# A chunked state recurrence with a squared-ReLU layer behind it: R loaded in runs of four tokens and turned on TensorE, the second correction in an accumulator of its own, the last decay row by an exponential, and a new order of all work

## The chip, the core and the metric

One core of one Trainium2 chip runs the whole program. The metric is device time in microseconds (us) of one execution. A core has five engines that work beside each other, each through its own list in order: TensorE (PE, with PEld for its weight loads), VectorE (DVE), ScalarE (ACT), GpSimd (POOL) and SyncE (SP, which here only issues DMAs). Sixteen DMA engines move the data that SP and POOL ask for.

## What is computed

For each of 4 batches and 8 heads a 40 x 40 state runs over 768 tokens, and each token's read-out goes into a two-matrix layer:

```python
for t in range(S):
    y[:, :, t] = np.einsum('bhd,bhde->bhe', rt, state)
    Sa = np.einsum('bhde,bhe->bhd', state, at)
    state_decay = state * wt[:, :, None, :] - np.einsum('bhd,bhe->bhde', Sa, bt)
    state = state_decay + np.einsum('bhd,bhe->bhde', vt, kt)
...
x = attn_out.transpose(0, 2, 1, 3).reshape(B * S, H * D)
out = np.maximum(x @ w_in, 0.0) ** 2 @ w_out
```

Inputs and output are float32; r, k, v, w, a, b are (4, 8, 768, 40), w_in is (320, 2048), w_out (2048, 320) and out (3072, 320).

## The kernel before

**Tiling.** The 768 tokens are cut into 6 chunks of 128. A *part* m = 0 to 23 is one chunk of one batch (m = 4c + batch) with all 8 heads; a *step* st = 0 to 47 is half a part (4 heads); a *unit* n = 0 to 47 is a quarter of the first matrix's work on two parts' tokens (in the groups of `SPLIT`, half of that on one part's); an *output* n = 0 to 23 is the 128 x 320 result of one part. Within a chunk the recurrence is done with triangular matrices in bf16; between chunks a state is handed on per batch.

**One part, in the order of its data.**

- Loads (`load`, L80 to L87): W, A, K, B, V and R of a part, each 160 KB as 128 tokens x 8 heads x 40 numbers, so in runs of 160 bytes. K and B share a tile NKB, R and V share NRV. Each tile has 4 buffers (`AHEAD`), and SP issues the loads in the order written.
- Decays: ln of W (`b_ln`, ACT), running sums on TensorE (`b_cs`), then exp of minus the sum (`b_xi`, GI), the sum less its own row (`b_cx`) and its exp (`b_gp`, GP). `b_gw` (L199) multiplies the last 32 token rows of W and GP on POOL or DVE; TensorE picks the last row out of that (`last_decay`).
- Scaled operands: `b_pk` (K and B times GI), `b_pa` (A times GP) into KBAp, and `b_cv` (L211, R and V cast to bf16 into RVp).
- Turning: K, B, A, R and V are needed with tokens along the free axis. For K and B this is done on TensorE in parts 0 to 19 (`b_kt`, 8 turns of 128 x 128, moved out by `b_kv`), for A in parts 0 to 7 (`b_ta`), for R and V in parts 0 to 7 (`b_rm`, 8 turns, moved out by `b_rv`). What is left goes by a DMA transpose that SP issues: `b_ka` (L252: A alone, 4 blocks, in parts 8 to 19, all of K, B and A, 12 blocks, in parts 20 to 23) and `b_rt` (L229: R and V, 8 blocks, parts 8 to 23).
- The solve: `st_a_mm` makes the triangular matrices, `st_a_ev` and `st_a_cut` move them out of PSUM and cut them (by a mask on DVE, or a copy on ACT and a cut on POOL). `b_p` starts an accumulator P, `b_m` moves it out, a first correction (`k1`) is added into P, `b_c1` takes the difference, a second correction (`k2`) is added into the same P, and `b_sn` moves the result out as SN. `b_x` (two POOL operations, L361 and L362) works out the size of the second correction for a check, `b_jk` and `st_energy` sum squares for that check on ACT.
- The read-out: `b_t`, `st_ex_mm`, `st_ex_ev` (EX), `st_z`, `st_kb` (uy), `st_y` (YN), `st_u` (the state handed on), `b_xt` and `b_xv` (the part's tokens turned for the layer, XS).

**The layer.** `f_r` and `f_m` (L543) multiply XS by w_in (WIN, loaded by POOL in ten pieces, `load_win`, two of which SP copies to a second half of the partitions, `twin_win`, L509); `f_e` (L563) takes the ReLU, `f_q` squares, `f_o` (L578) multiplies by w_out, `f_v` and `f_w` move the output out and store it.

**The end.** `sums` (L601) adds up the squares on TensorE, `verdict` (L605 to L618, DVE) compares them with bounds, and `get_flag` (L622) reads one flag into every engine; a branch (L885) follows. Two outputs (22 and 23) are moved out and stored behind the branch (`LAST`); the other side of the branch is a slow general path.

**The order.** Nothing is scheduled by the program's framework. `ORDER` is a text of some 1,900 tokens; each token issues one piece of work (`a.8@e1` is `st_a_mm` of step 8 into the PSUM banks e and 1, `pk.6:P` is `b_pk` of part 6 on POOL). The order of tokens gives the order on every engine, after a colon stands the engine, after @ the PSUM bank.

Of the kernel before, what the change touches and what calls it, by code (L numbers as in the profile page):

```python
# [18 lines left out]
def kernel(  # L19
# [62 lines left out]
    def load(key, m):  # L82
# [5 lines left out]

    NHC = 2 * NCH
    AN, AM, AC, AG, AI = 0, NBC, NBC + NHC, NBC + 2 * NHC, 2 * NBC + 2 * NHC  # L90
# [9 lines left out]
            for key, n in (("KBA", 4), ("G", 3), ("RV", 4))}  # L100
# [7 lines left out]
    def fill(k):  # L108
# [3 lines left out]
        elif k == 4:  # L112
            eng.memset(HM[:], 0.0)
            for u in range(2):
                eng.memset(HM[64 * u:64 * u + 64, :, u:u + 1], 1.0)
        elif k < 16:
            key, i = (("KBA", k - 5) if k < 9 else ("G", k - 9) if k < 12 else ("RV", k - 12))
            eng.memset(pads[key][i][:] if key == "G" else pads[key][i][:, :, :, D:64], 0.0)
        elif k < 19:
            eng.memset(SNs[k - 16][:, :, :, D:64], 0.0)  # L120
        else:
            eng.memset(UZs[k - 19][:], 0.0)
# [23 lines left out]
    HOME = {"f": {"tag": "ff", "bufs": 2}, "0": {"tag": "ca0"}, "1": {"tag": "ca1"},  # L146
# [51 lines left out]
    def b_gw(m):  # L198
        engine("gw", m).tensor_tensor(out=bt[m].G[LAST_T, 0, :, 0:D], op=ALU.mult,  # L199
                                      in0=nat.pop(("W", m))[LAST_T, 0], in1=bt[m].GP[LAST_T])  # L200
# [10 lines left out]
    def b_cv(m):  # L211
        move(pick["cv", m][0], bt[m].RV[:, :, :, 0:D], nat.pop(("RV", m))[:])
# [66 lines left out]
    CNs, Ps, TBs, uys, Mc, Cc, XSs = {}, {}, {}, {}, {}, {}, {}  # L279
# [26 lines left out]
    def cut_off(by, t_):  # L306
        if by == "A":
            nc.gpsimd.affine_select(  # L308
                out=t_, in_=t_, pattern=[[0, 2], [0, 2], [1, L]],
                compare_op=ALU.is_gt, fill=0.0, base=0, channel_multiplier=-1)  # L310

    def st_a_cut(st, s):
        cut_off(pick[f"av{s}", st][0], CNs[st][:, :, s])
# [22 lines left out]
    def b_m(m):  # L336
        c, bb = divmod(m, NB)
        if bb == 0:
            Mc[c] = chp.tile([128, NQ, 4, D], BF16, name="Mc", tag="Mc")
            Cc[c] = chp.tile([128, NQ, 4, D], BF16, name="Cc", tag="Cc")  # L340
        move(pick["m", m][0], part(Mc, m), flat(Ps[m]), -1.0)

    def corr(m, X, last):
        for h in range(NHH):
            nc.tensor.matmul(out=Ps[m][:, h // 2, h % 2, 0:D],  # L345
                             lhsT=CNs[m, "b"][:, h // 4, h // 2 % 2, h % 2, 1, :], rhs=X[:, h],
                             start=False, stop=last, skip_group_check=True)

    c1s = {}
# [5 lines left out]

    def b_sn(m):
        move(pick["s", m][0], flat(SNs[m % NSN]), flat(Ps.pop(m)), -1.0)

    def b_x(m):
        t_ = qdp.tile([128, NHH, D], FP32, name="x1", tag="x1", bufs=2)  # L360
        nc.gpsimd.tensor_tensor(out=t_[:], in0=part(Mc, m), in1=c1s.pop(m)[:], op=ALU.add)  # L361
        nc.gpsimd.tensor_tensor(out=part(Cc, m), in0=t_[:], in1=flat(SNs[m % NSN]), op=ALU.subtract)  # L362
# [7 lines left out]
    def st_energy(su):  # L370
        if su < 0 or su % 2 == 0:
            return
        hc = su // (NQ // 2)
        c, q = divmod(hc * (NQ // 2), NQ)
        src, at = ((Mc, AM), (Cc, AC))[su % (NQ // 2) // 2]
        jm = qdp.tile([128, NQ // 2, 4, D], BF16, name="jm", tag="jm", bufs=1)
        nc.scalar.activation(out=jm[:], in_=src[c][:, q:q + NQ // 2], func=ACTF.Square,
                             accum_out=ACC[:, at + hc:at + hc + 1])
# [43 lines left out]
    def st_ex_cut(st, s):  # L422
        cut_off(pick[f"ev{s}", st][0], EXs[st][:, :, s])
# [69 lines left out]
    def b_xv(m):  # L493
        c, b_ = divmod(m, NB)
        if b_ == 0:
# [25 lines left out]
    def unit(n):  # L521
        if n not in units:
# [3 lines left out]
            if jj == 0:  # L526
                Gts[h] = chp.tile([128, HB, NJ, L] if h in SPLIT else [128, NJ, HB, L], BF16,
                                  name="Gt", tag="Gt")
            if h in SPLIT:
                o.j0, o.per, o.bs = 8 * (jj % 2), 4, slice(b0 + jj // 2, b0 + jj // 2 + 1)  # L530
                o.Gt = Gts[h][:, jj // 2].rearrange("p j (a b) -> p j a b", a=1)
            else:
                o.j0, o.per, o.bs = 4 * jj, 2, slice(b0, b0 + HB)
                o.Gt = Gts[h][:]
            o.hp = [ps.tile([128, o.per, 4 // o.per, L], FP32, name="hp", **bank("fr", n, u))
                    for u in range(2)]
            o.begun = [0, 0]
        return units[n]

    def ffn_mm(o, u, i, g, rows):  # L540
        j = o.j0 + o.per * u + i
        o.begun[u] += 1
# [23 lines left out]
    def f_q(n):  # L566
        o = units[n]
        hs = o.hs[:].rearrange("p u x -> p (u x)")
        engine("q", n).tensor_tensor(  # L569
            out=o.Gt[:, o.j0:o.j0 + 2 * o.per].rearrange("p j a b -> p (j a b)"), in0=hs, in1=hs,  # L570
# [25 lines left out]
    def last_energy():  # L596
        st_energy(NS - 1)

# [4 lines left out]
    def verdict():  # L603
# [3 lines left out]
        nc.vector.memset(ok[:], 1.0)  # L607
        nc.vector.tensor_scalar(out=ok[:, AN:AN + NBC], in0=es[:, AN:AN + NBC], scalar1=1.5,
                                scalar2=None, op0=ALU.is_le)
        nc.vector.scalar_tensor_tensor(out=ok[:, AM:AM + NHC], in0=es[:, AM:AM + NHC],  # L610
                                       scalar=2.0 ** -16, in1=es[:, AC:AC + NHC],
                                       op0=ALU.mult, op1=ALU.is_ge)
# [8 lines left out]
    def get_flag():  # L621
# [4 lines left out]
        f.1:D lW.0 f.2:P lA.0 w.4@x w.11@0 f.4:D lW.1 f.20:D f.0:D f.9:D w.8@u lK.0 ln.0 f.16:D  # L626
# [292 lines left out]
```

## Time and profile before

| | |
|---|---|
| three runs, us | 257.33, 255.94, 257.05 (median 257.05) |
| the profiled execution, first to last instruction (its span) | 255.8 us |
| TensorE busy | 240.2 us (94%) |
| VectorE, ScalarE, GpSimd busy | 201.4, 206.3, 203.5 us |
| DMA | 184,467 packets, 38.44 MB, mean 150 GB/s |
| first matmul of the layer / last one | 38.7 us / about 251.3 us |

The profile gives no time for the profiled execution but its span; the median of the three runs lies 1.25 us above that span. Busy times are unions of instruction spans, so a busy share says how long an engine had something in it. Matmuls overlap one another in their spans. Of SP only what it issues and waits for is told.

### The profile page before, as it was taken

How to read it: one execution, taken by the hardware profiler on the slowest of the kernel's cores; microseconds unless marked ns; L12 is line 12 of the kernel's file. 1: busy time of each engine (PE TensorE's matmuls, PEld its weight loads, DVE VectorE, ACT ScalarE, POOL GpSimd, SP SyncE). 2: the span in 40 equal slices, each digit the busy share in tenths (PEclk: the TensorE clock that was granted, in tenths of full speed). 3: DMA queues.
4: the chain of work that ended last, by engine and by line, in shares of the span. 5: the costliest groups of instructions: out<-in, count | busy, mean ns of one | idle time of the engine just before them, and what ended most of it. 6: DMA issues, size and time to landing. Idle time of an engine off the chain costs nothing.

```text
span 255.8 us, 9549 instructions
## 1 busy us (share of the span) xinstructions
PE 240.2 (94%) x3893; PEld 193.8 (76%) x3893; DVE 201.4 (79%) x429; ACT 206.3 (81%) x470; POOL 203.5 (80%) x231
## 2 busy tenths in 40 slices
PE   7896787999999999999999999999998999799995
PEld 3464575899888888888888788888886877687872
DVE  4887798599999889899798898879797877575450
ACT  3598899499979898978999887889997868759821
POOL 6489787779989979999999999898896894197500
PEclk9999999799999999999999999999999999999999
DMA  7999998999988989999999977999999999540011
GB/s 130 189 153 187 166 180 149 168 168 163 169 157 153 155 146 163 164 186 190 148 171 172 201 137 142 166 152 209 150 158 162 186 179 130 118 120 28 28 55 62
DMA packets 184467, 38.44 MB, mean 150 GB/s; under 512 B 180064, under 2 KB 183136, under 8 KB 184416
## 3 DMA queue, kind: packets, MB, share of 16 engines
q1 hardware_dynamic: 183072, 35.14, 82.6%
q0 software_dynamic: 1344, 2.62, 6.1%
q8 instruction: 32, 0.52, 0.8%
q14 instruction: 19, 0.16, 0.2%
HBM read 28.84 MB, written 3.93 MB: 128 GB/s over the span
## 4 chain that ended last, share of the span: by engine, by line
PE 69%; DMA 15%; POOL 6%; SPq 5%; issue 2%; ACT 1%; DVE 0%; POOLq 0%
PE hp L543 20%; SPq L85 5%; DMA KBT<-KBAp 5%; PE cs L174 4%; PE ca L288 4%; PE ex L411 4%; PE tt L219 3%; PE uy L457 3%; PE P L345 2%; DMA WIN<-in_moe_w_in_dram 2%; DMA RV<-RVp 2%; PE uy L452 2%; DMA NA<-in_a_dram 2%; DMA WIN<-WIN 2%; DMA NKB<-in_b_dram 2%
## 5 line engine op out<-in xcount | busy, mean ns | idle before, releaser
L543 PE MATMUL hp<-XS,WIN 128*128 128x256 bf16 (+3 forms) x720 | 73.5, 255 | 2.0 <-DMA WIN<-WIN 2.0
L563 ACT ACTIVATE hs<-hp 128x512 bf16<-128x512 f32 x96 | 55.6, 600 | 15.7 <-PE hp L543 14.2
L543 PEld LDWEIGHTS <-WIN 128*128 128x128 bf16 (+1 forms) x720 | 49.6, 115 | 8.3 <-issue 3.6
L303 DVE TENSOR_TENSOR CN<-ca,MEX 128x512 bf16<-128x512 f32 x60 | 39.5, 683 | 8.8 <-PE ca L288 8.2
L578 PEld LDWEIGHTS <-Gt 128*128 128x128 bf16 x384 | 35.2, 97 | 12.3 <-issue 0.3
L303 DVE TENSOR_TENSOR EX<-ex,MEX 128x512 bf16<-128x512 f32 x60 | 39.9, 683 | 4.2 <-PE ex L411 3.9
L569 POOL TENSOR_TENSOR Gt<-hs 128x1024 bf16<-128x1024 bf16 x21 | 40.4, 1928 | 0.6 <-ACT hs L563 0.3
L308 POOL TENSOR_SCALAR_AFFINE_SELECT CN<-CN 128x512 bf16<-128x512 bf16 x36 | 24.9, 698 | 10.9 <-ACT CN L301 7.8
L308 POOL TENSOR_SCALAR_AFFINE_SELECT EX<-EX 128x512 bf16<-128x512 bf16 x36 | 24.8, 703 | 6.6 <-ACT EX L301 5.1
L569 DVE TENSOR_TENSOR Gt<-hs 128x1024 bf16<-128x1024 bf16 x27 | 22.3, 830 | 5.3 <-ACT hs L563 4.5
L366 ACT ACTIVATE jk<-CN 128x1024 bf16<-128x1024 bf16 x24 | 25.6, 1068 | 0.2
L301 ACT ACTIVATE CN<-ca 128x512 bf16<-128x512 f32 x36 | 21.0, 594 | 4.9 <-PE ca L288 4.6
L203 POOL TENSOR_TENSOR KBAp<-NKB,GI 128x640 bf16<-128x640 f32 x14 | 22.2, 1582 | 2.1 <-DMA NKB<-in_b_dram 1.1
L208 POOL TENSOR_TENSOR KBAp<-NA,GP 128x320 bf16<-128x320 f32 x18 | 16.2, 900 | 7.2 <-ACT lnW L169 3.1
L301 ACT ACTIVATE EX<-ex 128x512 bf16<-128x512 f32 x36 | 20.6, 600 | 1.4 <-PE ex L411 1.1
L362 POOL TENSOR_TENSOR Cc<-x,SN 128x320 bf16<-128x320 f32 x24 | 20.1, 837 | 1.9
L457 PE MATMUL uy<-KBAp,EX 128*128 128x40 bf16 x384 | 21.3, 181 | 0.0
L288 PE MATMUL ca<-KBT 64*128 64x128 bf16 x384 | 17.9, 220 | 3.1 <-DMA KBT<-KBAp 2.1
L199 POOL TENSOR_TENSOR Gp<-NW,GP 32x320 bf16<-32x320 f32 x20 | 18.3, 920 | 2.9 <-issue 1.5
L361 POOL TENSOR_TENSOR x<-Mc,c 128x320 f32<-128x320 bf16 x24 | 20.0, 832 | 0.3
L473 DVE TENSOR_TENSOR YN<-uy,GP 128x224 bf16<-128x224 f32 (+1 forms) x48 | 16.5, 347 | 4.2 <-PE uy L457 4.2
L457 PEld LDWEIGHTS <-EX 128*128 128x128 bf16 x384 | 17.9, 96 | 0.9 <-issue 0.3
(151 smaller groups left out, 613.0 us busy)
## 6 DMA issues: line engine op xcount, KB each, us to landing
NW<-in_w_dram SPq DMA_DIRECT2D x24, 160.0 KB, 3.9
NA<-in_a_dram SPq DMA_DIRECT2D x24, 160.0 KB, 4.0
NKB<-in_k_dram SPq DMA_DIRECT2D x24, 160.0 KB, 4.0
NKB<-in_b_dram SPq DMA_DIRECT2D x24, 160.0 KB, 4.1
NRV<-in_v_dram SPq DMA_DIRECT2D x24, 160.0 KB, 4.0
NRV<-in_r_dram SPq DMA_DIRECT2D x24, 160.0 KB, 4.0
out_dram<-osb SPq DMA_DIRECT2D x24, 160.0 KB, 2.8
WOUT<-in_moe_w_out_dram POOLq DMA_DIRECT2D x2, 640.0 KB, 7.6
```

The lines of the kernel that those rows point to most:

```text
L203: engine("pk", m).tensor_tensor(out=bt[m].KB[:, 0:2, :, 0:D], in0=nat.pop(("KB", m))[:], op=ALU.mult, in1=bt[m].GI[:].rearrange("p (u h) e ...
L288: nc.tensor.matmul(out=ca[s][:, i, u, :], lhsT=o.KBT[half(s), u, j0 + i, :], rhs=o.KBT[half(s), 2, j0 + i, :], start=(i == 0 and u == 0), ...
L301: nc.scalar.activation(out=out, in_=in_[:], func=ACTF.Copy)
L303: nc.vector.tensor_tensor(out=out, in0=in_[:], op=ALU.mult, in1=MEX[:].rearrange("p (i u) x -> p i u x", u=2))
L308: nc.gpsimd.affine_select(out=t_, in_=t_, pattern=[[0, 2], [0, 2], [1, L]], compare_op=ALU.is_gt, fill=0.0, base=0, channel_multiplier=-1)
L362: nc.gpsimd.tensor_tensor(out=part(Cc, m), in0=t_[:], in1=flat(SNs[m % NSN]), op=ALU.subtract)
L366: nc.scalar.activation(out=jk[:], in_=CNs[m, "b"][:].rearrange("p x i s u t -> p (x i s) u t")[:, :, 1, :], func=ACTF.Square, accum_out=AC ...
L457: nc.tensor.matmul(out=uy[:, (2 * i + s) * D:(2 * i + s + 1) * D], lhsT=EXs[st][:, i, s, u, :], rhs=o.KB[:, u, 2 * (j0 + i) + s, 0:D], sta ...
L543: nc.tensor.matmul(out=o.hp[u][:, i], lhsT=inner(g, rows, j), rhs=XSs[o.c][rows, g, o.bs, :], start=(o.begun[u] == 1), stop=(o.begun[u] > ...
L563: nc.scalar.activation(out=o.hs[:, u], func=ACTF.Relu, in_=o.hp[u][:].rearrange("p j a b -> p (j a b)"))
L569: engine("q", n).tensor_tensor(out=o.Gt[:, o.j0:o.j0 + 2 * o.per].rearrange("p j a b -> p (j a b)"), in0=hs, in1=hs, op=ALU.mult)
L578: nc.tensor.matmul(out=ops[n][:], rhs=WOUT[:, j, :], lhsT=Gts[h][:, b_, j, :] if h in SPLIT else Gts[h][:, j, b_, :], start=(j == 0), stop ...
```

## The change

- **R.** R gets a tile of its own (NR) and is read by two DMAs of 80 KB, one for the even and one for the odd heads, in runs of four tokens (640 bytes). The partitions then hold (head pair, block of 32 token groups). `b_cr` casts it with a rearrangement, four TensorE turns per part (`b_rm`, now in all 24 parts) bring it to the layout needed, and `b_rv` moves it out with a second rearrangement. V alone is cast by `b_cv`; it is turned on TensorE in parts 0 to 6 (`b_vm`, `b_vv`) and by a DMA transpose of 4 blocks in parts 7 to 23.
- **Second correction.** It goes into a PSUM tile Q of its own. `b_xf` moves -P out in float32, `b_sn` subtracts Q from it on DVE (24 times), the check's sum of squares is taken from Q directly on ACT (`b_ec`, 24 of 320 columns), and `b_x` with its two POOL operations is gone. `b_em` keeps the sum of squares over the first move.
- **Last decay row.** `b_gw` is an exponential of 32 rows of the running sum on ACT, in all 24 parts. The tile of W is thereby free after `b_ln`.
- **K and B** are turned on TensorE in parts 0 to 15 (before: 0 to 19); from part 16 on K, B and A go by the DMA transpose of 12 blocks.
- **Cuts** (`aq`, `eq`) have an engine of their own in the order: 56 on POOL and 27 on DVE (before: 72 on POOL). Squares (`f_q`): 37 on POOL and 11 on DVE (before 21 and 27).
- **Order.** `ORDER` is another text; the PSUM banks of the tag `ff` are named one by one (f and g).

The diff, cut to its core:

```diff
+    def load_r(m):
+        c, bb = divmod(m, NB)
+        nat["R", m] = natp.tile([128, 2, TI, D], FP32, name="NR", tag="NR")
+        for s in range(2):
+            nc.sync.dma_start(
+                out=nat["R", m][:, s].rearrange("p i e -> p (i e)"),
+                in_=r[bb].rearrange("(j s) t e -> s j t e", s=2)[s, :, c * L:(c + 1) * L, :]
+                .rearrange("j (b i) e -> j b (i e)", i=TI))
...
     def b_gw(m):
+        if pick["gw", m][0] == "A":
+            nc.scalar.activation(out=bt[m].G[LAST_T, 0, :, 0:D], in_=bt[m].cs[LAST_T], func=ACTF.Exp)
...
     def b_cv(m):
-        move(pick["cv", m][0], bt[m].RV[:, :, :, 0:D], nat.pop(("RV", m))[:])
+        move(pick["cv", m][0], bt[m].RV[:, 1, :, 0:D], nat.pop(("V", m))[:, 0])
+
+    def b_cr(m):
+        move(pick["cr", m][0], bt[m].RV[:, 0].rearrange("p (i s) e -> p s i e", s=2)[:, :, :, 0:D],
+             nat.pop(("R", m))[:])
...
     def b_rm(m):
-        bt[m].t1 = turned(bt[m].RV, **bank("rm", m))
+        bt[m].t1 = turned(bt[m].RV, us=(0,), **bank("rm", m))
...
     def b_rv(m):
-        move(pick["rv", m][0], bt[m].RVT[:], bt[m].t1[:])
+        move(pick["rv", m][0], bt[m].RVT[:, 0].rearrange("p j (b i) -> p i j b", i=TI),
+             bt[m].t1[:, 0].rearrange("p i (j b) -> p i j b", j=PB))
...
         nc.sync.dma_start_transpose(
-            out=o.RVT[:].rearrange("p u j t -> p (u j) t"),
-            in_=o.RV[:].rearrange("p u h e -> p (u h e)"))
+            out=o.RVT[:, 1], in_=o.RV[:, 1].rearrange("p h e -> p (h e)"))
...
+    def b_xf(m):
+        x1s[m] = qdp.tile([128, NHH, D], FP32, name="x1", tag="x1", bufs=2)
+        move(pick["xf", m][0], x1s[m][:], flat(Ps[m]), -1.0)
+
+    def b_k2(m):
+        Qs[m] = ps.tile([128, PB, 2, 64], FP32, name="Q", **bank("k2", m))
+        corr(m, Qs[m], c1s.pop(m), True)
+
     def b_sn(m):
-        move(pick["s", m][0], flat(SNs[m % NSN]), flat(Ps.pop(m)), -1.0)
-
-    def b_x(m):
-        t_ = qdp.tile([128, NHH, D], FP32, name="x1", tag="x1", bufs=2)
-        nc.gpsimd.tensor_tensor(out=t_[:], in0=part(Mc, m), in1=c1s.pop(m)[:], op=ALU.add)
-        nc.gpsimd.tensor_tensor(out=part(Cc, m), in0=t_[:], in1=flat(SNs[m % NSN]), op=ALU.subtract)
+        nc.vector.tensor_tensor(out=flat(SNs[m % NSN]), in0=x1s.pop(m)[:], in1=flat(Qs[m]),
+                                op=ALU.subtract)
...
+    def b_ec(m):
+        energy(flat(Qs[m]), NHH * D, AC + m)
...
-        ep.0@f rb.44 o1.20@0 o2.21 q.44:D es.0 ov.21:D fa.47 ra.47 o2.20 o1.23@f rb.47 ov.20:D
-        o1.22@f q.47:D o2.22 o2.23 w.17@0 ow.21 ow.20 w.5@e w.18@s gw.21:P fl.0
+        q.46:D ra.47 q.47:P o1.22@e o2.22 o1.23@u o2.23 w.5@f ep.0@s ow.20 ow.19 w.18@x ov.21:A
+        ow.21 w.17@0 ow.18 es.0 fl.0
```

What this moves, at three places. **First, SP near the copies of w_in's pieces.** SP's list before (NA, NW, NKB, NRV are the parts' tiles, WIN1 the pieces that are copied):

```order
L85 DMA NA_612<-in_a_dram 128x8x40
L85 DMA NKB_625<-in_k_dram 128x8x40
L85 DMA NKB_625<-in_b_dram 128x8x40
L509 DMA WIN1_107<-WIN1_107 64x1024
L85 DMA NA_725<-in_a_dram 128x8x40
L85 DMA NKB_737<-in_k_dram 128x8x40
L85 DMA NRV_745<-in_v_dram 128x8x40
L85 DMA NKB_737<-in_b_dram 128x8x40
L509 DMA WIN1_107<-WIN1_107 64x1024
L85 DMA NRV_745<-in_r_dram 128x8x40
```

And SP's list now, at the same copies (NR is the new tile of R, NV that of V):

```order
L86 DMA NA_544<-in_a_dram 128x8x40
L86 DMA NW_546<-in_w_dram 128x8x40
L86 DMA NKB_548<-in_b_dram 128x8x40
L86 DMA NKB_548<-in_k_dram 128x8x40
L542 DMA WIN1_109<-WIN1_109 64x1024
L94 DMA NR_552<-in_r_dram 128x1x160 x2
L86 DMA NV_555<-in_v_dram 128x8x40
L94 DMA NR_557<-in_r_dram 128x1x160 x2
L542 DMA WIN1_109<-WIN1_109 64x1024
L86 DMA NV_561<-in_v_dram 128x8x40
```

The first copy stands behind 29 loads before and behind 33 now, four of these 33 being R's in two halves; between the copies stand four loads before and three now.

**Second, TensorE at the end.** Before, around the sums of squares (`ep`; Gt and WOUT belong to the second matrix, op_ is an output):

```order
L578 LDWEIGHTS Gt
L578 MATMUL op__6139<-WOUT,Gt 128x320
L601 MATMUL ep<-ACC,ones_f 1x96
L578 LDWEIGHTS Gt
L578 MATMUL op__6151<-WOUT,Gt 128x320
```

Now (`wu` is a filler matmul on ones):

```order
L610 MATMUL op__6377<-WOUT,Gt 128x320
L149 LDWEIGHTS ones_b
L149 MATMUL wu<-ones_b 128x512
L149 LDWEIGHTS ones_b
L149 MATMUL wu<-ones_b 128x512
L630 MATMUL ep<-ACC,ones_f 1x108
```

Before, 64 matmuls of the layer follow `ep` (56 of outputs 20 to 23 and 8 of a unit); now the last matmul of the last output stands ahead of it.

**Third, DVE at the end.** Before (`es` to `bad` is the check, `osb` an output moved out, TENSOR_LOAD the reading of the flag):

```order
L569 TENSOR_TENSOR Gt<-hs 128x1024 x5
L605 COPY es<-ep 1x96
L607 MEMSET ok 1x96
L608 TENSOR_SCALAR ok<-es 1x24
L610 SCALAR_TENSOR_TENSOR ok<-es 1x12
L613 TENSOR_SCALAR ok<-es 1x48
L616 TENSOR_REDUCE nok<-ok 1x1
L618 TENSOR_SCALAR bad<-nok 1x1
L158 COPY osb<-op__6139 128x320
L158 COPY osb<-op__6151 128x320
L569 TENSOR_TENSOR Gt<-hs 128x1024
L622 TENSOR_LOAD bad
```

Now:

```order
L170 COPY osb<-op__6242 128x320
L601 TENSOR_TENSOR Gt<-hs 128x1024 x2
L634 COPY es<-ep 1x108
L636 MEMSET ok 1x108
L639 TENSOR_TENSOR ec<-es 1x12
L640 SCALAR_TENSOR_TENSOR ok<-es,ec 1x12
L643 TENSOR_SCALAR ok<-es 1x24
L645 TENSOR_SCALAR ok<-es 1x48
L648 TENSOR_REDUCE nok<-ok 1x1
L650 TENSOR_SCALAR bad<-nok 1x1
L654 TENSOR_LOAD bad
```

The check has one operation more, and no work of the layer stands between it and the reading of the flag.

More of the change, by code (lines that the diff above doesn't have):

```diff
@@ L494, in b_xv @@
         c, b_ = divmod(m, NB)
[L495 removed]
+        if c not in XSs:
             XSs[c] = chp.tile([128, NG, NB, L], BF16, name="XS", tag="XS", bufs=3)
@@ L812 @@
     STEP = 8
+    held = [bank("o1", int(tok.split(".")[1].split(":")[0])) for tok in LAST.split()
+            if tok.startswith("ov.")]
+    spare = [x for x in HOME.values() if x not in held]
     def general():
```

391 lines of the change are left out of this document (199 added, 192 removed).

## The prediction

> **What bounds the kernel now.** I read the page's head, then the span cut into stages (columns: span, busy us and instructions of PE, PEld, DVE, ACT, POOL, then granted clock, DMA share, GB/s), then in each stage who waits and the chain that ended last.
>
> ```profile
> span 255.8 us, 9549 instructions
> 0.00:46.00 46.00, 37.06 (x558) 25.04 (x559) 35.36 (x81) 34.12 (x74) 34.19 (x55) 1.00 0.98 163
> 46.00:190.00 144.00, 143.71 (x2476) 121.66 (x2473) 126.20 (x267) 127.22 (x299) 133.67 (x139) 0.99 0.99 166
> 190.00:220.00 30.00, 26.82 (x451) 21.88 (x451) 22.10 (x45) 22.77 (x51) 20.50 (x25) 1.00 1.13 166
> 220.00:251.40 31.40, 31.39 (x411) 24.88 (x409) 17.71 (x40) 21.81 (x48) 15.12 (x15) 1.00 0.20 55
> 251.40:255.80 4.40, 1.23 (x6) 0.38 (x4) 0.00 (x0) 0.41 (x1) 0.00 (x0) 1.00 0.24 82
> ```
>
> Five stages. Up to 46 us PE is empty for 8.9 us, and much of the rest is filler, while the DMA engines are full (0.98): this stage ends when the data are in. From 46 to 190 us PE is never empty (143.71 of 144) and nothing shorter than PE's list can help, though DMA is full too (0.99) and POOL close (133.67). From 190 to 220 us PE is empty for 3.2 us with DMA over full. Up to 251.4 us PE works off the layer alone. The last 4.4 us are the end of the program. So only the first, third and last stage can give or take much, and PE's own work in between.
>
> In the first stage the chain and PE's waits read:
>
> ```profile
> 34.25 5.96 DMA WIN<-in_moe_w_in_dram
> 40.23 4.71 DMA WIN<-WIN
> ```
>
> ```profile
> PE hp L543 <- DMA WIN<-WIN: 2.0, 1, 2.0
> ```
>
> ```profile
> 45.50:49.00 3.50, 3.50 (x55) 3.45 (x53) 1.65 (x5) 1.62 (x4) 3.23 (x5) 0.51 1.09 189
> ```
>
> The layer waits 2.0 us for the second copy of a piece of w_in, and right behind it PE runs 3.5 us at a granted clock of 0.51, which loses 3.5 x 0.49 = 1.7 us.
>
> **R's loads.** What does a load cost where DMA is full?
>
> ```profile
> q1 hardware_dynamic: 183072, 35.14, 82.6%
> q0 software_dynamic: 1344, 2.62, 6.1%
> ```
>
> ```profile
> 240.00:256.00 16.00, 12.61 (x112) 8.80 (x109) 5.09 (x14) 5.34 (x12) 0.05 (x1) 1.00 0.14 48
> ```
>
> ```profile
> NRV<-in_r_dram SPq DMA_DIRECT2D x5, 160.0 KB, 4.7
> ```
>
> q1: 0.826 x 16 engines x 255.8 us / 183,072 = 18.5 ns for a packet of 192 bytes on average. A load of 160 KB in runs of 160 bytes is 1,024 packets: 1,024 x 18.5 / 16 = 1.18 us. No row shows 640 bytes. Below: 18.5 ns, 256 packets, 0.30 us a load. Above: by bytes at q0's price (0.061 x 16 x 255.8 / 1,344 = 186 ns for 1,949 bytes), 61 ns, 0.98 us. Nearest: from 240 us on almost only stores of 1,280 bytes run, 0.14 x 16 x 16 us for 48 GB/s x 16 us = 600 packets, so 60 ns. On the line between 192 bytes at 18.5 and 1,280 at 60, 640 bytes take 35.6 ns and a load of R 0.57 us. I take that: 0.61 us saved a load (0.20 to 0.88).
>
> The Trainium skill (DMA: Bandwidth & Descriptors, "Specifications") says that transfers of 512 bytes and more go at line rate, about 27 GiB/s per engine. That would be 22 ns for 640 bytes, an estimate, 4.2 us instead of the 3.1 below, and 253.5 us in the end. The stores' 1,280 bytes in 60 ns (21 GB/s) do not reach that rate, so I stay with the line.
>
> *First stage:* five loads of R are issued by 46 us (row above), so the same data are in 5 x 0.61 = 3.1 us earlier (1.0 to 4.4). The copies of w_in now stand behind pieces that POOL asks for first, and ahead of the pieces that need no copy; that may take away the 2.0 us and with it the 1.7 us of half clock, or another first-time wait may take their place (0 to 3.7): half, 1.8 us. Together **-4.9** (-1.0 to -8.1).
>
> **Turns on PE.** Before: 20 x 8 for K and B, 8 x 4 for A, 8 x 8 for R and V, 256. Now: 16 x 8, 8 x 4, 24 x 4 for R, 7 x 4 for V, 284.
>
> ```profile
> 51.33 0.45 PE tt L219 x8
> ```
>
> 28 more at 0.45 / 8 = 56 ns are **+1.6** us on an engine that is never empty; nothing hides them. (Both ends: 0 if they fall into empty PE time before 46 us, 1.6.) The Trainium skill (TensorE: Matmul & The Clock Gate, "Part 4: PE-mode transpose") holds that turns don't count as busy for the clock and run at the slow one. By that the 28 would cost twice as much, an estimate of 3.1 us, and the end 256.1; but the row's 56 ns at granted clock 1.00 are 128 columns at full speed, so the trace speaks against it here.
>
> **The other engines** are not what ends the middle stage, so what they gain or lose costs nothing as long as they stay below PE. The prices:
>
> ```profile
> L569 POOL TENSOR_TENSOR Gt<-hs 128x1024 bf16<-128x1024 bf16 x21 | 40.4, 1928 | 0.6 <-ACT hs L563 0.3
> L362 POOL TENSOR_TENSOR Cc<-x,SN 128x320 bf16<-128x320 f32 x24 | 20.1, 837 | 1.9
> L199 POOL TENSOR_TENSOR Gp<-NW,GP 32x320 bf16<-32x320 f32 x20 | 18.3, 920 | 2.9 <-issue 1.5
> L361 POOL TENSOR_TENSOR x<-Mc,c 128x320 f32<-128x320 bf16 x24 | 20.0, 832 | 0.3
> ```
>
> ```profile
> L154 ACT ACTIVATE SN<-P 128x320 bf16<-128x320 f32 x18 | 7.9, 436 | 3.7 <-PE P L345 2.6 <-issue 1.0
> L377 ACT ACTIVATE jm<-Cc 128x640 bf16<-128x640 bf16 x12 | 8.8, 734 | 0.2 <-POOL Cc L362 0.2
> L180 ACT ACTIVATION_READ_ACCUMULATOR GI<-cs 128x1 f32 x24 | 5.0, 208 | 0.0
> ```
>
> POOL loses 40.1 (L361, L362) and 18.3 (L199) and gains 16 squares x 1.93 = 30.9: at least 27 us less, on the engine that was fullest in the middle. ACT gains 24 exponentials of 32 rows, priced like SN<-P (24 x 0.44 = 10.5), and 24 sums of squares (24 x 0.64 = 15.5), and loses 8.8 + 2.4 with jm<-Cc; the moves of casts and evictions nearly cancel. **ACT +14** in all, some 9.6 of it in the middle's 144 us (144 / 205 of the time after 46 us): 127.2 becomes 137, still under 144. I cost it at 0; what hides it is PE's list, and the cover is gone where ACT's 16.8 us of empty time can't be used (a rival). The second correction's own accumulator adds no matmul; its move and subtraction take the place of one move. A load of R is two issues now, but no longer shares a tile with V.
>
> **Third stage.** PE's waits, and the pieces of the chain:
>
> ```profile
> PE ca L288 <- DMA KBT<-KBAp: 2.1, 2, 1.4
> PE ex L411 <- DMA RV<-RVp: 1.1, 1, 1.1
> ```
>
> ```profile
> 188.66 5.88 DMA RV<-RVp
> 202.99 6.36 DMA KBT<-KBAp
> 213.40 5.26 DMA KBT<-KBAp
> ```
>
> All 3.2 us of empty PE are DMA transposes that land late in a full queue. R no longer goes that way (4 blocks instead of 8), the queue carries 24 x 0.61 = 14.6 us less up to there, but K, B and A go by 12 blocks from part 16 instead of 20. Between 0 and all of the 3.2, nearer to all: **-2.4** (-3.2 to +3.2, the rise if the eight full transposes each wait as the last four do).
>
> **The end.** Rows of PE, DVE, ACT and of the flag's readers:
>
> ```profile
> 242.85 0.33 PE L601 MATMUL ep<-ACC,ones_f 128*1 128x96 f32 x2
> 244.52 0.24 DVE L605 COPY es<-ep 1x96 f32<-1x96 f32 x1
> 245.55 0.14 DVE L618 TENSOR_SCALAR bad<-nok 1x1 int32<-1x1 f32 x1
> 250.08 1.25 PE L578 MATMUL op__6200<-WOUT,Gt 128*128 128x320 bf16 x8
> 251.37 0.44 ACT L154 ACTIVATE osb<-op__6200 128x320 f32<-128x320 f32 x1 [0.60 <-PE op__6200 L578]
> 251.17 1.46 PE L137 MATMUL wu<-ones_b 128*128 128x512 bf16 x6
> ```
>
> ```profile
> L622 ACTq TENSOR_LOAD <-bad x1: 464/464/464, 245.9 to 245.9; - x1
> L622 SPq FUSED_REGOPS  x1: 183/183/183, 248.5 to 248.5; - x1
> ```
>
> Before, the check lay under the last outputs, and the last copy out began 0.04 us behind the last matmul (250.08 + 1.25 to 251.37). Now everything stands in a row behind it: two fillers (2 x 1.46 / 6 = 0.49), `ep` 0.33, `es` to `bad` 245.69 - 244.52 = 1.17 and one operation more (0.17), the flag 0.46, the branch about as long as SP's 0.18, then output 22's copy (0.44), which waits behind the branch too, ahead of the last one: 3.24 - 0.04 = **+3.2** (2.6 without the fillers' and branch's part, 4.0 with a wait between every two).
>
> **Sum** against the profiled span: 255.8 - 4.9 + 1.6 - 2.4 + 3.2 = 253.3. The median lies 1.25 above the span: **254.5 us**.
>
> **Rivals.**
> 1. *ACT becomes the bound of the middle.* For it: this wait of ACT can't be filled by more ACT work if the order has it at fixed places; ACT was already 88% full.
>
> ```profile
> ACT hs L563 <- PE hp L543: 14.2, 18, 2.8
> ```
>
> Against it: POOL, fuller still, left PE without a gap. If all 16.8 us of ACT's empty time stay, the middle takes 9.6 us longer: 262.9, as a time 264; it decides once more than 7.2 us (144 - 136.8) of empty time stay. Slower. 15%.
> 2. *The transposes of parts 16 to 23 wait twice as much*: the third term is +3.2 instead of -2.4: 260.1. Slower. For it the share of 1.13, against it the 14.6 us less in the queue. 12%.
> 3. *The longer runs are priced by bytes*, so the change hardly does what it says: five loads save 1.0 instead of 3.1 and the queue is as full in the third stage: 254.5 + 2.1 + 2.4 = 259.0. 12%.
> 4. *DMA, not PE, sets the pace all through* (share 0.98 and 0.99): then all 14.6 us come off and 255.8 - 14.6 + 1.6 + 3.2 + 1.25 = 247.3. Against it: PE without a gap for 144 us. 13%.
>
> **How the numbers follow.** The forecast, 252 to 257 us, has 48%. Half a per cent of 257.05 is 1.3 us, about what a measurement of this kernel can tell from no change, so faster is under 255.8 and slower over 258.3. Faster: three quarters of the forecast and rival 4, 0.48. Slower: rivals 1 and 2, most of 3, a little of the forecast, 0.34. The range leaves out half of rivals 1 and 4 and a little more: 247.5 to 261.5.
>
> **What would show it.** The first layer matmuls dense some 4 to 5 us sooner, and no half clock at 45 us; 284 turns; ACT near 220 us busy and POOL near 176; in the last 60 us waits of PE for KBT and RV well under 3.2 us; the check behind the last matmul and about 7.6 us from that matmul to the span's end. Wrong would be PE empty in the middle with ACT as the one waited for, R's loads landing no sooner, or a check that starts earlier than the list says.

## The result, and the profile after

The changed kernel takes **297.32 us** (median of 294.70, 295.51, 299.14 and 301.56) against 257.19 us before. Two of these four ran in a slower state (299.14 and 301.56 us), and every comparison from here on leaves such executions out, which makes 295.1 us here, 37.9 over before and a ratio of **1.147** (95% interval 1.138 to 1.156). Forecast were 254.5 us in a range of 247.5 to 261.5. The profiled execution has a span of 293.0 us, 37.2 more than before.

The page's head and first table:

```profile
span 293.0 us, 9683 instructions
PE 249.9 (85%) x3921; PEld 197.0 (67%) x3921; DVE 221.7 (76%) x466; ACT 227.0 (77%) x529; POOL 178.2 (61%) x192
```

No engine is full any more: PE falls from 94% to 85%, and none of the others has risen above the share that it had before. The stages (columns as in the prediction):

```profile
0.00:46.00 46.00, 34.82 (x455) 23.17 (x455) 31.61 (x79) 33.53 (x79) 29.01 (x50) 0.93 0.91 159
46.00:190.00 144.00, 128.50 (x2198) 105.23 (x2197) 121.03 (x255) 125.03 (x291) 95.33 (x99) 0.99 0.89 146
190.00:281.60 91.60, 84.92 (x1267) 68.21 (x1266) 67.85 (x126) 67.66 (x160) 53.89 (x45) 1.00 0.54 96
281.60:293.00 11.40, 1.65 (x8) 0.40 (x6) 1.18 (x8) 0.77 (x2) 0.00 (x0) 0.69 0.12 37
```

In the same 144 us of the middle PE starts 2198 matmuls instead of 2476 and is empty for 15.5 us instead of 0.3. The DMA share fell from 0.99 to 0.89.

Where the 37.2 us lie follows from two marks, the first matmul of the layer and the end of the last output's matmuls. Rows of the layer's tile and of the chain:

```profile
L571 PE MATMUL hp<-XS,WIN x720: 214/269/421, 44.0 to 275.9; 128*128 128x256 bf16 x72, 128*128 128x128 bf16 x48, 64*128 64x256 bf16 x36, 64*128 64x128 bf16 x24
```

```profile
279.40 2.17 PE op__6377 L610 x16
281.57 0.43 PE wu L149 x2
282.01 0.29 PE ep L630 x2
...
283.46 0.15 DVE bad L650
...
283.63 0.47 ACTq L654
...
284.16 0.05 ACTq L920
284.21 3.70 issue
...
288.05 0.06 ACT osb L166
```

The start takes 44.0 instead of 38.7 us (**+5.3**), the end 293.0 - 281.57 = 11.4 instead of 255.8 - 251.33 = 4.5 us (**+6.9**; 251.33 is 250.24 + 1.09 of before's last output), and what lies between 237.6 instead of 212.6 us (**+25.0**).

**The start.** The chain there:

```profile
12.55 5.20 DMA NR<-in_r_dram
18.52 1.50 POOL KBAp L218
20.05 0.54 ACT GI L192 x2
20.61 0.49 DVE cx L197
21.10 0.94 DVE KBT L170 x2
22.09 1.03 PE ca L313 x13
```

```profile
PE ca L313 <- DVE KBT L170: 6.0, 2, 5.4
```

```profile
22.00:24.00 2.00, 1.92 (x26) 1.32 (x27) 1.19 (x4) 1.06 (x4) 0.60 (x2) 0.50 1.34 182
24.00:26.00 2.00, 2.00 (x13) 1.26 (x12) 1.90 (x4) 1.60 (x3) 1.99 (x5) 0.50 1.40 172
```

R's first loads are needed early now, since R is cast on POOL ahead of part 2's scaling of K and B; that scaling waits in POOL's list, ACT's GI waits for a buffer that it frees, DVE's cx waits for GI, and PE stands for 5.4 us behind the move that follows cx. cx needs nothing of GI; both only read the tile cs, a pattern that returns in the middle. Behind the gap PE runs at a granted clock of 0.50 for 4 us. The half clock forecast to go from 45 us has moved to 22 us.

**The middle.** PE's own waits are short and many; what tells more are the waits of the engines that serve it, ACT and DVE:

```profile
ACT hs L591 <- PE hp L571: 5.2, 6, 2.1
ACT junk L397 <- DVE SN L392: 5.1, 3, 2.9
ACT x L166 <- DVE c L380: 4.7, 5, 2.2
```

```profile
DVE cx L197 <- ACT GI L192: 12.8, 5, 5.1
DVE SN L392 <- ACT junk L397: 5.1, 6, 1.9
DVE c L380 <- ACT x L166: 4.4, 5, 1.2
```

Before, ACT waited for PE (14.2 us at the layer). Now ACT and DVE wait for each other: `x` (-P in float32) and `c` only read P, and `junk` (the square) and SN only read Q, yet the two never run side by side on two engines. Rows of two places, ACT's and then DVE's:

```profile
86.77 0.43 ACT L397 ACTIVATE junk<-Q 128x320 bf16<-128x320 f32 x1
...
97.45 0.44 ACT L166 ACTIVATE x<-P 128x320 f32<-128x320 f32 x1 [0.77 <-DVE c L380]
```

```profile
87.32 0.49 DVE L392 TENSOR_TENSOR SN<-x,Q 128x320 bf16<-128x320 f32 x1 [0.55 <-ACT junk L397]
...
96.94 0.47 DVE L380 SCALAR_TENSOR_TENSOR c<-P,Mc 128x320 bf16<-128x320 f32 x1
```

SN begins 0.12 us behind the square's end, `x` 0.04 us behind `c`'s. In all 24 parts the square and SN stand at least 0.03 us apart, and so do `c` and `x` in the 18 where two engines do them. Which of the two waits goes by the order: SN begins behind the square in 8 of the 24 parts, and the square behind SN in 16; `c` behind `x` in 8 of the 18, `x` behind `c` in 10. So in 8 parts the change put a square of 0.43 us into the chain from Q to SN, which the diff doesn't say. The Trainium skill (PSUM — Partial Sum Buffer, "Terms") does: two engines may not be on one bank at once, reads against reads included. The trace agrees, with the waits above. The prediction did not weigh that rule.

DVE's largest wait is of the same kind: cx waits 12.8 us for GI, though both only read cs. Before, cx began ahead of GI in 21 of 24 parts; in the changed kernel it does so in 14.

Another thing in these lists is how long R's turned blocks take to move out:

```profile
L166 ACT ACTIVATE RV<-tt x19: 636/1329/1455, 24.0 to 239.2; 128x512 bf16<-128x512 bf16 x19
L170 DVE COPY RV<-tt x12: 408/1296/1339, 13.7 to 252.2; 128x512 bf16<-128x512 bf16 x12
```

```profile
L166 ACT ACTIVATE KBT<-tt 128x512 bf16<-128x512 bf16 x2 | 1.2, 590 | 0.0
L170 DVE COPY KBT<-tt 128x512 bf16<-128x512 bf16 x6 | 2.5, 418 | 0.9 <-PE tt L238 0.9
```

The first two rows give the shortest, middle and longest of 19 and 12 moves, 7 of them plain ones of V: 1.33 us on ACT and 1.30 on DVE in the middle. The same shape takes 0.59 us (ACT) and 0.42 us (DVE) in plain order. The Trainium skill (SBUF — State Buffer, "Door 1: The DMA port swizzle") holds that steps of up to 8 bf16 cost nothing; this move writes every fourth one and takes about twice as long on ACT and three times as long on DVE. If the step is what costs, page and measurement differ, and the measurement decides.

### The profile page after: what moved, and what is told of

It reads as the page before. It is cut to its first block, busy times and chain, and to the rows that moved or that the text cites. A ratio compares the mean times of both kernels' runs of the same rounds, so it can differ in the third digit from the quotient of the medians.

```text
span 293.0 us, 9683 instructions
## 1 busy us (share of the span) xinstructions
PE 249.9 (85%) x3921; PEld 197.0 (67%) x3921; DVE 221.7 (76%) x466; ACT 227.0 (77%) x529; POOL 178.2 (61%) x192
## 4 chain that ended last, share of the span: by engine, by line
PE 28%; ACT 24%; DVE 19%; issue 9%; SPq 7%; DMA 7%; POOL 5%; ACTq 0%; POOLq 0%; DVEq 0%
PE hp L571 7%; SPq L86 5%; ACT hs L591 5%; ACT RV L166 3%; DVE EX L328 3%; DMA NV<-in_v_dram 3%; DVE CN L328 3%; ACT jk L402 2%; ACT Gp L212 2%; ACT CN L326 2%; DMA NR<-in_r_dram 2%; PE ca L313 2%; POOL Gt L601 2%; ACT GI L192 2%; DVE RV L170 2%
## 5 line engine op out<-in xcount | busy, mean ns | idle before, releaser
L601 POOL TENSOR_TENSOR Gt<-hs 128x1024 bf16<-128x1024 bf16 x37 | 70.8, 1919 | 29.0 <-ACT hs L591 28.9
L591 ACT ACTIVATE hs<-hp 128x512 bf16<-128x512 f32 x96 | 54.6, 606 | 10.7 <-PE hp L571 5.2
L328 DVE TENSOR_TENSOR EX<-ex,MEX 128x512 bf16<-128x512 f32 x53 | 34.9, 684 | 4.6 <-PE ex L444 3.7
L218 POOL TENSOR_TENSOR KBAp<-NKB,GI 128x640 bf16<-128x640 f32 x17 | 26.8, 1574 | 11.1 <-PE uy L289 3.8
L333 POOL TENSOR_SCALAR_AFFINE_SELECT CN<-CN 128x512 bf16<-128x512 bf16 x26 | 17.1, 661 | 19.5 <-ACT CN L326 13.5
L326 ACT ACTIVATE EX<-ex 128x512 bf16<-128x512 f32 x43 | 25.2, 624 | 3.0 <-PE ex L444 3.0
L333 POOL TENSOR_SCALAR_AFFINE_SELECT EX<-EX 128x512 bf16<-128x512 bf16 x30 | 20.1, 677 | 12.2 <-ACT EX L326 6.5
L166 ACT ACTIVATE RV<-tt 128x512 bf16<-128x512 bf16 x19 | 24.1, 1266 | 0.1
L197 DVE TENSOR_TENSOR cx<-cs,lnW 128x320 f32<-128x320 f32 x24 | 11.6, 483 | 16.4 <-ACT GI L192 12.8
L313 PEld LDWEIGHTS <-KBT 64*128 64x128 bf16 x384 | 12.8, 96 | 15.4 <-DVE KBT L170 6.0
L186 PE MATMUL cs<-lnW,UTI 128*128 128x320 f32 x48 | 18.0, 460 | 0.7 <-ACT Gp L212 0.3
```

The costliest lines, as they stand in the source:

```text
L166: nc.scalar.activation(out=out, in_=in_, func=ACTF.Copy, scale=scale or 1.0)
L218: engine("pk", m).tensor_tensor(out=bt[m].KB[:, 0:2, :, 0:D], in0=nat.pop(("KB", m))[:], op=ALU.mult, in1=bt[m].GI[:].rearrange("p (u h) e ...
L313: nc.tensor.matmul(out=ca[s][:, i, u, :], lhsT=o.KBT[half(s), u, j0 + i, :], rhs=o.KBT[half(s), 2, j0 + i, :], start=(i == 0 and u == 0), ...
L326: nc.scalar.activation(out=out, in_=in_[:], func=ACTF.Copy)
L328: nc.vector.tensor_tensor(out=out, in0=in_[:], op=ALU.mult, in1=MEX[:].rearrange("p (i u) x -> p i u x", u=2))
L333: nc.gpsimd.affine_select(out=t_, in_=t_, pattern=[[0, 2], [0, 2], [1, L]], compare_op=ALU.is_gt, fill=0.0, base=0, channel_multiplier=-1)
```

## The experiments

All times are medians; "over" is the median less that of the kernel before in the same comparison. The changed kernel is 37.9 us over. It was timed in a comparison of its own, and the ratios' intervals are about 0.008 (2 us) to either side, so a difference between kernels of two comparisons is good to about 3 us, an estimate from these intervals.

**1. Is it R's rearranged move, the late check, R's runs, or ACT's load?** Four kernels, each the changed one with one edit.

```diff
 x1_flat
-        move(pick["rv", m][0], bt[m].RVT[:, 0].rearrange("p j (b i) -> p i j b", i=TI),
-             bt[m].t1[:, 0].rearrange("p i (j b) -> p i j b", j=PB))
+        move(pick["rv", m][0], bt[m].RVT[:, 0], bt[m].t1[:, 0])
 x2_early
-  fa.47 fa.46 o2.21 ra.46 rb.46 q.46:D ... o2.23 w.5@f ep.0@s ow.20 ... ow.18 es.0 fl.0
+  fa.47 ep.0@e fa.46 o2.21 ra.46 rb.46 es.0 q.46:D ... o2.23 w.5@f ow.20 ... ow.18 fl.0
 x3_short
-        natp.tile([128, 2, TI, D], FP32, name="NR", tag="NR")
+        natp.tile([128, 2, TI, D + 8], FP32, name="NR", tag="NR")
 x4_noec
-        energy(flat(Qs[m]), NHH * D, AC + m)
+        pass
```

> The changed kernel with R's turned blocks moved out in their plain order (the second rearrangement left out, so R's tokens stand in the wrong order and the output isn't the reference's; same bytes, same instructions). Theory A, the rearranged move: it takes 1.3 us instead of about 0.6 us, 24 times, on ACT (17) and DVE (7), and holds up everything behind it in two lists that are served in order. Then RV<-tt falls to about 0.6 us (ACT) and 0.42 us (DVE), 18 us of engine time go, and the span falls from 293 by 10 to 20 us. Theory B, the order: the new list couples the engines at fixed places whatever this move costs; the span stays above 288 us. Theory C, ACT's amount of work: ACT loses 12 of 227 us and the span falls by no more than 12 us.

289.18 us, ratio 1.120 (1.109 to 1.132), 30.6 over: **7.3 us** less. The moves fell to 0.61 (ACT) and 0.42 us (DVE), as theory A has it, but the span only to 287.5, 5.5 less than 293.0 and under A's 10 to 20. Theory C allows that too; x4 tests it.

> The changed kernel with the check's sums and the flag ahead of the last outputs, as before (all is computed). Theory: the end is a row of waits behind the last matmul: two fillers, sums, verdict, reading of the flag, and 3.7 us of branching that stood under the last outputs before. Then 7 us go, and from the last matmul of the last output to the span's end it takes about 4.4 us instead of 11.4. By the prediction's working the row is worth 3.2 us. Rival: the wait on the flag's branch stays exposed since the flag is read at the same place of each list, and under 1 us goes.

291.89 us, 1.127 (1.117 to 1.136), 33.3 over: **4.6 us** less. From the last output's matmuls to the span's end it takes 290.5 - 285.35 = 5.1 us instead of 11.4, 6.3 less. So the late row is worth 5 to 6 us, not 3.2. The difference is the branch, and it is TensorE's. Rows of the changed kernel, then one of before:

```profile
L920 ACTq COMPARE_BRANCH  x1: 50/50/50, 284.2 to 284.2; - x1
L920 PEldq COMPARE_BRANCH  x1: 3537/3537/3537, 284.2 to 284.2; - x1
```

```profile
ACT osb L166 <- PEq L920: 10.0, 1, 10.0
```

```profile
L885 PEldq COMPARE_BRANCH  x1: 3493/3493/3493, 250.2 to 250.2; - x1
```

ACT's own branch takes 0.05 us; the 3.70 us in its chain end when PE's sequencer is through its branch of 3.54 us. Before, that branch was as long, but ACT's two copies began at 250.33 and 251.37 us, ahead of its end. Why ACT's copies wait for it in the changed kernel was not separated.

> The changed kernel with R loaded in runs of 160 bytes again (each run goes to a slot of 48 numbers, so that no two join; all else as it is, all is computed). By the prediction a load of 160 KB costs 0.61 us more of the 16 engines in runs of 160 bytes than in runs of 640, 14.6 us in all: the share of the queue rises by about 5 points of the span, and the first stage ends about 3 us later. If the changed kernel's pace is set by engines that wait for one another and not by DMA, the time stays within 3 us; if it is set by the data, it rises by 5 to 15 us.

310.54 us, 1.203 (1.195 to 1.210), 52.0 over: **14.1 us** more. So R's longer runs are worth some 14 us in the changed kernel, though not in the way the prediction priced. The queue's rows:

```profile
q1 hardware_dynamic: 160896, 34.22, 69.0%
```

```profile
q1 hardware_dynamic: 179328, 34.22, 63.8%
```

That is 0.690 x 293.0 = 202 us of all 16 engines in the changed kernel and 0.638 x 308.4 = 197 us with 18,432 packets more: the queue's time has not grown. What has grown is SP's time for an issue, from 0.58 to 1.26 us in the median of 48:

```profile
L94 SPq DMA_DIRECT2D NR<-in_r_dram x48: 528/584/1992, 9.8 to 232.2; - x48
```

```profile
L94 SPq DMA_DIRECT2D NR<-in_r_dram x48: 543/1256/2868, 9.9 to 247.9; - x48
```

POOL's waits for R's data at its casts grow from 6.6 to 11.3 us. That this brings the 14 us was not separated.

> The changed kernel without the sum of squares over the second correction (24 squares of 128x320 and 24 readings of the sum on ACT, 16 us in all; the check then sees zeros). Theory C, ACT's amount of work bounds the kernel: the span falls by 12 to 16 us. Theory A or B: ACT is 77 per cent busy and waits in many places, so it falls by 2 to 8 us, less than by the plain move of R if A holds.

293.13 us, 1.135 (1.126 to 1.143), 34.6 over. 16 us less work on ACT bring 3.3 us, not told from nothing (the intervals overlap). ACT's amount of work, theory C, is not the bound.

**2. Is it the data, or the order?**

```diff
 y1_after_noload, y2_before_noload
+        if m >= AHEAD:
+            nat[pair, m] = held[pair, m % AHEAD]
+            return
 y3_reload (loads alone at other places, here part 10's of V; its cast is cv.10)
-  rt.9 lW.12 lV.11 ... lV.10 cv.10:P
+  z.12@x lV.10 fa.10 kb.12 k1.8 rm.9@s ... cv.10:P
 y4_before_r (before; R's path as in the change, part 8's tokens)
-  cv.8:A ... rt.8
+  cv.8:A cr.8:A ... rm.8@0 ... rv.8:D ... rt.8
```

> The changed kernel with the loads of parts 4 to 23 left out (their work is done on the data of parts 0 to 3, so the output isn't the reference's; 120 of 144 loads go, everything else stays in its place). Theory D, late data: the new list issues many loads only a few places ahead of the cast or scaling that needs them, and what waits for them on POOL, DVE and ACT is what PE waits for. Then nearly all of the loss in the middle goes: the span falls from 293 to 255 to 268 us. Theory B, the list's order on the computing engines: the span falls by less than 10 us.

297.26 us, 1.155 (1.148 to 1.161), 39.8 over: no gain. **Theory D falls**; the data of parts 4 to 23 does not set the changed kernel's pace.

> The kernel before with the same 120 loads left out (parts 4 to 23 work on the data of parts 0 to 3). By the prediction's reading PE is never empty from 46 to 190 us and only the third stage's 3.2 us and a part of the start are the data's: the span falls by 3 to 10 us. If data set the pace of before too (the prediction's fourth rival), it falls by 15 us or more.

252.46 us, 0.979 (0.973 to 0.984), 5.1 under. The 120 loads of parts 4 to 23 together are worth 5.1 us of before. This is the ceiling of whatever shorter loads of these parts could bring there, and it closes the fourth rival (247.3): in the middle the DMA share falls from 0.99 to 0.34.

> The changed kernel with SP's loads of parts 6 to 23 put at other places of the list: each as soon as its buffer is free, at most 90 places ahead of its first use (now 1 to 338 places ahead, several within 10); no other work is moved and all is computed. Theory D: the span falls by more than 10 us. Theory B: it stays within 5 us of 293.

303.13 us, 1.177 (1.169 to 1.184), 45.6 over: evenly placed loads cost 7.7 us more. Both theories missed it, and the cause is open; POOL waits less for loads, but ACT waits 8.0 us for W instead of 1.8.

> The kernel before, in its own order, with R's path of the change alone: R loaded in runs of four tokens into a tile of its own, cast and moved out with the two rearrangements, turned on TensorE in all parts (4 turns, put into gaps of the PSUM banks for parts 8 to 23; moved out by ACT in odd and DVE in even parts), V by the DMA transpose of 4 blocks. If R's path is itself the cost (rearranged moves, 64 more turns, a longer way from load to read-out), it takes 270 us or more. If the order is the cost (theory B or D), it stays within 254 to 264 us.

277.10 us, 1.074 (1.067 to 1.081), **19.6 over**. R's path alone, in the old order, costs 20 us as placed here, 3.2 of them ahead of the layer's first matmul (at 41.9 us, before at 38.7). PE's middle stage there:

```profile
46.00:190.00 144.00, 131.45 (x2257) 109.58 (x2254) 121.85 (x247) 120.01 (x275) 119.67 (x133) 1.00 0.82 142
```

DVE and ACT are no fuller in the middle than before (126.20 and 127.22), and still PE does 2257 matmuls instead of 2476: it is where the work stands and how long one piece holds its list, not the sum.

**3. The other parts alone, and all parts in the old order.** In z3 and z5 the fill of a buffer clears part 1's last decay row again, so part of the output isn't the reference's.

```diff
 z1_before_r_flat = y4 with x1's edit
 z2_second (before; part 10's tokens)
-  c.10 kb.18 k2.10 ... s.10:A ... x.10
+  xf.10:A c.10 kb.18 k2.10 ec.10 ... s.10
 z3_gw (before)
-  gw.3:P
+  xi.3 gw.3:A
 z5_all_old = y4 + z2 + z3, and for parts 16 to 19
-  kt.17@s kv.17:D ... ka.17
+  pa.17:P ka.17
```

> The kernel before with R's path of the change in its own order (as in y4), but R's turned blocks moved out in their plain order (the second rearrangement left out, so the output isn't the reference's). If the cost of R's path is the length of that move (1.1 to 1.2 us instead of 0.4 to 0.6, 24 times, on lists that PE waits for), most of the 20 us go: under 267 us. If it is what the path adds at all (72 turns, casts and moves at places where PE waits), it stays above 272 us.

267.23 us, 1.040 (1.027 to 1.052), 8.9 over, 10.7 less than y4. Just over half of R's path is the length of that one move.

> The kernel before, in its own order, with the second correction of the change alone (P moved out in float32 ahead of it by ACT, in six parts DVE; P's tile started anew; the difference on DVE; its square sums on ACT, 24 instead of 12; the two POOL operations gone). By the prediction it adds no matmul and costs nothing. If PE's density hangs on what DVE and ACT finish in time, the 24 moves and 24 squares on ACT (16 us more than went) cost something: 2 to 10 us.

279.06 us, 1.083 (1.069 to 1.097), **20.7 over**, far outside both guesses; 4.8 of them lie ahead of the layer's first matmul (at 43.5 us). As placed here, the second reader stands ahead everywhere: SN begins behind the square in all 24 parts, and `c` behind `x` in all 18 where two engines do them, against 8 and 8 in the changed kernel. (The second correction also reuses P's tile here instead of taking one of its own.) So this is the price of this placing, and not that of the part in the changed kernel. ACT waits at the square that stands right behind the correction, and SN waits for the square:

```profile
ACT junk L370 <- PE P L344: 18.3, 17, 3.5
...
DVE c L352 <- ACT x L154: 10.3, 9, 2.6
DVE SN L365 <- ACT junk L370: 6.9, 12, 1.0
```

PE's middle stage, with DVE and ACT less busy than before again:

```profile
46.00:190.00 144.00, 133.24 (x2293) 110.37 (x2291) 121.19 (x261) 117.40 (x284) 96.94 (x99) 1.00 0.93 155
```

> The kernel before, in its own order, with the last decay row by an exponential on ACT alone, right behind GI's (24 of 0.43 us; POOL and DVE lose 20 us). By the prediction it costs nothing. If ACT's list is what PE waits for, it costs 2 to 8 us.

259.99 us, 1.010 (0.994 to 1.026), 1.7 over: not told from nothing. One of its four executions took 566.11 us and is not in this median; its cause is open.

> All parts of the change but the new order, in the order of before: R's path (as in y4), the second correction (as in z2), the exponential (as in z3), and K and B by the DMA transpose from part 16 on. The cuts, the squares and the check at the end stand as before. If the new order is the cause of the loss in the middle, this takes 255 to 270 us. If the added work is, it takes 280 us or more, and at least the sum of y4, z2 and z3 over before.

311.34 us, 1.210 (1.197 to 1.223), 53.0 over: more than the changed kernel, and more than y4, z2 and z3 together (42.0). So the new order alone is not the cause, as **theory B** has it: the work added costs this much in the old order as placed here, 15.1 us more than in the new one. As z2 shows, the placing is itself an order; what the same work costs in the old order with the second readers behind was not tried.

**4. Taking the costs out of the changed kernel, one after the other.**

```diff
 w1_nosecond (with x4's edit)
-        x1s[m] = qdp.tile([128, NHH, D], FP32, name="x1", tag="x1", bufs=2)
-        move(pick["xf", m][0], x1s[m][:], flat(Ps[m]), -1.0)
-        nc.vector.tensor_tensor(out=flat(SNs[m % NSN]), in0=x1s.pop(m)[:], in1=flat(Qs[m]), ...
+        move("D", flat(SNs[m % NSN]), flat(Qs[m]), -1.0)
 w2 = w1 + x1's edit;  w3 = w2 + x2's edit;  w5 = z2 with x4's edit
 v1_noturn = w3, and rm and rv only for m < 4;  v2_noturn_noload = v1 + y1's edit
```

> The changed kernel without the second correction's extra readers: the move of -P in float32 and the sum of squares over Q are left out, and SN is taken from Q alone (so the output isn't the reference's); all matmuls and the order stay. Theory E, second readers: the profile shows that P and Q are never read by two engines at once (SN starts 0.03 us or more after the square's end in all 24 parts), so each second reader stands in the chain from P to SN, and what waits behind on PE, ACT and DVE with it. Then it falls from 297 to 275 to 285 us, far more than without the square alone (293). Rival, amount of work: ACT loses 24 of 227 us and DVE 3; no more than 8 us go.

290.36 us, 1.129 (1.121 to 1.137), 33.6 over: 4.3 us less, as the rival has it and not theory E's 12 to 22. What is expected above of all 24 parts holds for z2; in the changed kernel SN begins behind the square in 8, and there the second readers cost little.

> w1, and R's turned blocks moved out in their plain order too (as in x1). If the costs of the two parts add, 7 to 10 us less than w1. If one lies in the shadow of the other, less than 4 us.

285.47 us, 1.113 (1.106 to 1.119), 28.7 over: 4.9 less than w1, between the two guesses.

> w2, and the check ahead of the last outputs (as in x2): 5 to 7 us less than w2. What then is left over the 257 us of before is the new order, the 24 more turns with their banks, and the rest: under 268 us if the three parts are the cause, over 275 if most of it is something else.

280.38 us, 1.090 (1.085 to 1.096), 23.7 over: 5.1 less, and over 275: more than half is something else.

> The second correction alone in the old order (as in z2), without the sum of squares over the result (left out: the check sees zeros). Theory E: SN no longer stands behind ACT's square, and ACT no longer waits at it (18 us there in z2); of the 21 us that z2 lost 10 to 15 go: 264 to 269 us. Rival, amount of work: ACT's list gets 16 us shorter, but was no fuller than before; at most 5 us go.

269.76 us, 1.048 (1.043 to 1.054), 13.0 over: 7.7 us of z2's 20.7 hang on the square over the result, between theory E's 10 to 15 and the rival's 5. The other second reader is still in the chain, `c` behind `x` and PE behind `c`:

```profile
DVE c L352 <- ACT x L154: 8.7, 8, 1.4
...
PE P L344 <- DVE c L352: 3.6, 5, 1.4
```

How much of the 13.0 us is its share was not separated.

> w3, and R's turns and the moves behind them left out from part 4 on (the read-outs use R of the part four before, so the output isn't the reference's). If R's turns on PE and their moves hold up the lists, 8 to 15 us less than w3 (in the old order R's path with a plain move costs 10 us over before). If what is left is the order, less than 5 us.

275.73 us, 1.068 (1.061 to 1.076), 18.4 over: 5.3 less than w3, at the edge of the second case.

> v1, and the loads from part 4 on left out as well. Before with these loads left out takes 252.5. If late data come to bound the kernel once the other costs are gone, 8 us or more less than v1; if not, within 4 us of v1. What then stays over 252.5 is the new order's and the start's.

271.28 us, 1.050 (1.042 to 1.059), 13.9 over, 4.5 less than v1: with the other costs out of the way data counts again, as before. Against y2, which has the same loads left out, 18.8 us stay.

So of the 37.9 us, in the changed kernel: second correction's readers 4.3, rearranged move 4.9, late check 5.1, R's turns with their moves 5.3, data 4.5, each given the ones ahead of it. The 13.9 us left, more than a third, are not settled. 3.5 us of the 18.8 over y2 lie before the first matmul of the layer (40.9 against 37.4 us), whose rows are below; the rest is in the order on PE, ACT and DVE, the exponential and the cuts on DVE, which were not told apart. One candidate that no run took out: DVE's cx still waits 10.7 us for GI in v2.

```profile
L577 PE MATMUL hp<-XS,WIN x720: 215/269/304, 40.9 to 257.5; 128*128 128x256 bf16 x72, 128*128 128x128 bf16 x48, 64*128 64x256 bf16 x36, 64*128 64x128 bf16 x24
```

```profile
L547 PE MATMUL hp<-XS,WIN x720: 215/269/304, 37.4 to 241.6; 128*128 128x256 bf16 x72, 128*128 128x128 bf16 x48, 64*128 64x256 bf16 x36, 64*128 64x128 bf16 x24
```

None of the kernels that still compute the whole output beat before.

## Why the prediction was wrong, point by point

- **The step that failed: "The other engines are not what ends the middle stage, so what they gain or lose costs nothing as long as they stay below PE."** A sum of busy time below PE's does not hide work that stands between two pieces of PE's work. In the changed kernel's middle DVE, ACT and POOL are all less busy than before (121.0, 125.0 and 95.3 us against 126.2, 127.2 and 133.7), and PE is empty for 15.5 us. y4 and z2 cost 20 us each, as placed there, with DVE and ACT no fuller in the middle than before. The argument from POOL (fuller still, and PE without a gap) doesn't carry over; a likely reason, not tested, is that POOL held much work asked for early, while the change puts its work between P and SN and between R's turn and the read-out.
- **"The moves of casts and evictions nearly cancel"**: they don't. R's move takes 1.33 us on ACT (a plain one 0.59), and ACT rose by 20.7 us, not 14. DVE, which had no sum at all, rose by 20.3. POOL fell by 25.3, as worked out (27).
- **"The second correction ... adds no matmul; its move and subtraction take the place of one move"**: true of the count, but its second readers of P and Q never run beside the first ones. 20.7 us alone in the old order, with every second reader ahead; 4.3 in the new.
- **First stage, -4.9**: came out as +5.3. R's longer runs do not shorten the queue (x3: the 0.61 us saved a load are not there), the 120 loads of parts 4 to 23 are worth 5.1 us of before (y2), and the first cast of R holds up part 2's scaling on POOL.
- **Turns on PE, +1.6**: the row's 56 ns hold, but a turn also needs a bank and a move; R's 80 turns and 20 moves from part 4 on cost 5.3 us together (v1).
- **Third stage, -2.4**: right in kind, as far as this shows: PE, held up elsewhere, waits 1.8 us for transposes in all now, which doesn't price the term:

```profile
PE ex L444 <- DMA RV<-RVp: 1.6, 1, 1.6
...
PE ca L313 <- DMA KBT<-KBAp: 0.2, 1, 0.2
```

- **The end, +3.2**: right in kind, 6.9 in the profile, 4.6 by x2 and 5.1 by w3. The term mis-sized is the branch. It was taken as 0.18 us from a row of SP that isn't a branch; TensorE's branch takes 3.54 us, and ACT's copies wait 3.70 for it.
- **The rivals.** The first, ACT as the bound (264 us, 15%), had the side right and the mechanism half: PE does wait for the lists behind it, but ACT's load alone is not it (x4), and the price was far off. The third, R's runs priced by bytes, is what the queue shows. The second and the fourth fell.

## What to carry to other kernels

Where one engine is dense, ask of each added operation not whether its engine has time left but whether it stands between two pieces of the dense engine's work, in lists served in order: here two parts that kept the sums of DVE and ACT below PE's cost 20 us each in one placing. Count the readers of a PSUM tile: here two on different engines never ran side by side, and the order decided which of them stood in the chain. Before a change that saves transfers, leave the transfers out: what that brings (here 5 us) is all that can be had.

## What the runs showed of the hardware that was not expected

- A move out of PSUM that writes every fourth bf16 took about twice as long as a plain one of the same size on ACT and three times as long on DVE: 1.33 and 1.30 us in the middle of all, against means of 0.61 and 0.42 us in x1.
- The branch on the flag took TensorE 3.54 us and ACT 0.05 us (before: 3.49 and 0.05).
- 18,432 packets more in runs of 160 instead of 640 bytes added nothing to the queue's time; SP's time for an issue doubled, and the kernel took 14.1 us more.
- Two readers of one PSUM tile on two engines never overlapped: square and SN in 24 of 24 parts, `x` and `c` in 18 of 18, GI and cx in 24 of 24.
